# A linear-attention kernel with routed experts: the second copy of one head by a transfer of its own, for units 3 to 7

## The chip, the cores and the metric

The kernel runs on one core of a Trainium2 chip, in one launch. The metric is the device time of the whole program in microseconds (us). Beside the times there is a profile: one execution recorded by the hardware profiler. The engines are called as in its rows: PE (TensorE's matmuls) and PEld (its weight loads), DVE (VectorE), ACT (ScalarE), POOL (GpSimd) and SP (SyncE, which here only issues transfers). A "q" behind a name (SPq, PEldq) marks an entry of that engine's sequencer, such as the issue of a transfer or a wait on a semaphore.

## What is computed

An RWKV-5 attention over 4 batches, 8 heads, 768 steps and 48 channels a head, and behind it a mixture of 8 experts in which every expert gets the same number of tokens:

```python
for t in range(S):
    kt, vt, rt = (k[:, :, t], v[:, :, t], r[:, :, t])
    cur = np.einsum('bhd,bhe->bhde', u[None] * kt, vt)
    y[:, :, t] = np.einsum('bhd,bhde->bhe', rt, state + cur)
    state = w[None, :, :, None] * state + np.einsum('bhd,bhe->bhde', kt, vt)
...
logits = x @ w_gate                      # x: y as 3072 rows of 384
order = np.argsort(-logits.flatten())    # best pairs of token and expert first
...                                      # a token takes the expert while it has room (384 places)
h = np.maximum(x[mask] @ w1[e], 0.0)     # 384 -> 1024
out[mask] = h @ w2[e]                    # 1024 -> 384
```

All data are float32. `r` stands for the receptances, `k` for the keys, `v` for the values, `w` for the decays.

## The kernel before, in words

The attention is done in 24 units: a unit is one batch and one chunk of 128 steps, and the units go chunk by chunk, four batches (`B` = 4) in each. The class `Mild` does this part, and the order of its work is written out by hand in `run`: step `n` of its loop does the main work of unit `n` and prepares units `n+1` to `n+5`. Each engine, and each queue of transfers, works its instructions off in that order.

Keys and receptances lie in `krs`, a ring of five buffers. A buffer holds ten places of 64 channels for each of the two (`H + 2` places, 48 of the 64 channels used): places 0 to 7 are the eight heads, and place 8 (`H`) holds a second copy of head 4 (`HP`). The helper `pair` makes pairs of heads for the transposes on PE: places (0,1), (2,3), (5,6) and (7,8). So the fourth pair needs the second copy, and PE's transposes of a unit end with it. POOL's product of the keys with the decays (`keys`, line 436, into `kss`) reads places 0 to 3 and 5 to 8, so it needs the second copy of the keys too; POOL's product of receptances and keys (`own`, lines 442 and 443, into `rk`) reads places 0 to 7 alone.

The steps that the change and the prediction touch:

- `load(n, what)`, line 336: SP issues one transfer for the keys, receptances or values of a unit, 128 rows of 8 heads, 192 bytes each, 192 KB. `start` issues those of units 0 to 4 (values: 0 to 3) ahead of everything; step `n` begins with the keys and receptances of unit `n+5` and the values of unit `n+4`.
- `again_one(n, x)`, line 344: ACT copies head 4 of a unit's keys (x = 0) or receptances (x = 1) into place 8. It is used for units 0 to 7: for units 0 to 2 ahead of the loop, for units 3 to 7 in steps 0 to 4. From unit 8 on, `again` (line 340) does the same for both on DVE.
- `diagonal` (line 495): ACT writes the diagonal of a unit's matrix `AT`, eight small instructions a unit; `own_sum` (line 448, DVE) sums what it writes.
- `turn(n)`: PE transposes the (scaled) keys and the receptances (line 458); ACT copies the one (line 475), DVE scales the other (line 477).
- `pairs` (line 505): 32 matmuls of keys against receptances into `g_ps`, and the masked copy of them on DVE (line 512).
- `outputs`: matmuls into `y_ps` (line 545), `keep` (line 524) for the state, and ACT's copy of the result (line 564). `rows` transposes a result (line 595), ACT copies it (line 604), and SP stores it (line 605).
- `gate_weights` (line 404): in step 2, behind the loads of that step, SP issues two transfers of 6 KB that bring the gate's weights `wgp`. They are first read in step 4 by `gate` (line 575), PE's product of the four results of a chunk with these weights; it comes behind `pairs` of that step and ahead of `outputs`.

Behind the attention, the tokens are assigned to experts by a search on DVE, gathered by POOL, and sent through the experts' two layers by PE.

Of the kernel before, what the change touches and what calls it, by code (L numbers as in the profile page):

```python
# [21 lines left out]
T = 128  # L22
# [4 lines left out]
def attention_any(ctx, tc, r, k, v, w, u, wg, x_dram, LG, ident, walk):  # L27
# [52 lines left out]
    nc.scalar.dma_start(u_bc, u.rearrange("h d -> (h d)").partition_broadcast(128))  # L80
    nc.scalar.dma_start(wg_sb, wg.rearrange("(f p) e -> p f e", p=128))
    load(0)
    load(1)

    pw = const.tile([128, HP, T], F32, name="pw")
# [54 lines left out]
    def scale(n):  # L140

        load(n + 2)
        kt, rt, vt = loaded.pop(n)
        c = units[n][1]
# [130 lines left out]
class Mild:  # L275
# [52 lines left out]
    def load(self, n, what):  # L328
        if n >= self.N:
            return  # L330
        nc, H, D = self.nc, self.H, self.D
        b, c = self.units[n]
        for x in what:
            t = self.vts[:, n % self.NV] if x == "v" else self.krs[:, n % self.NK, "kr".index(x)]
            src = {"k": self.k, "r": self.r, "v": self.v}[x]
            nc.sync.dma_start(t[:, 0:H, 0:D], src[b, :, ts(c, T), :].rearrange("h s d -> s h d"))

    def again(self, n):
        kr, HP, H, D = self.krs[:, n % self.NK], self.HP, self.H, self.D
        self.nc.vector.tensor_copy(kr[:, :, H, 0:D], kr[:, :, HP, 0:D])  # L340
# [278 lines left out]
    def run(self, step):  # L619
        N, B, C, walk = self.N, self.B, self.C, self.walk  # L620
        self.live = {n: {} for n in range(N)}
        self.start()
        u_ps = self.spread_u()
        self.again_one(0, 0)
        k0 = self.keys_turned(0, True)
        self.again_one(0, 1)
        self.idle(2, "g_ps")
        r0 = self.r_turned(0)
        self.copy_u(u_ps)
        self.own(0)  # L630
        self.scaled(0, "k", k0, "pieces")
        self.scaled(0, "r", r0, "pieces")
        self.table(self.WK, "k")
        self.again_one(1, 0)
        self.table(self.WR, "r")
        self.again_one(1, 1)
        self.idle(2, "g_ps")
        k1 = self.keys_turned(1, True, walk.ps, "few")
        wk_ps = self.wk_turned()
        r1 = self.r_turned(1, walk.ps, "counts")  # L640
        self.wk_table(wk_ps)
        self.scaled(1, "k", k1, self.WK)
        self.own_sum(0)
        self.diagonal(0, (0,))
        self.again_one(2, 0)
        self.diagonal(0, (1,))
        self.again_one(2, 1)
        self.scaled(1, "r", r1, self.WR)
        self.own(1)
        self.keys(0)  # L650
        self.own_sum(1)
        nc, AB = self.nc, self.ones8
        nc.vector.tensor_mul(self.chunk, AB[:, 0, :, 1, 8], AB[:, 0, :, 1, 8])
        self.pairs(0)
        self.diagonal(1)
        self.own(2)
        chores = walk.constants()
        for n in range(N):
            self.load(n + 5, "kr")
            self.load(n + 4, "v")  # L660
            if n == 2:
                self.gate_weights()
            soon, split, full = n <= B, 0 < n < 3, n >= B and n % B == 0
            halves = ((0,), (1,)) if split or full else ((0, 1), ())
            if n == 0:
                self.turn(2, True)
                self.own_sum(2)
                self.idle(3, "y_ps")
                self.pairs(1)
                self.keys(1)  # L670
            else:
                step(n, "first")
                if not soon and n + 3 < N:
                    self.again(n + 3)
                if n == 2:
                    self.own_sum(n + 2)
                if split:
                    self.keep(n - 1)
                    self.pairs(n + 1)
                if n + 2 < N:  # L680
                    if n != 2 and n + 3 < N:
                        self.own_sum(n + 2)
                    self.turn(n + 2, between=lambda: step(n, "turning"))
                if n <= N - B:
                    self.rows((n - 1,), "few")
            if soon:
                self.again_one(n + 3, 0)
            if n + 2 < N:
                self.diagonal(n + 2, halves[0])
            if soon:  # L690
                self.again_one(n + 3, 1)
            if n > 2:
                step(n, "turned")
                if n <= B:
                    self.keep(n - 1)
                if n + 1 < N:
                    self.pairs(n + 1, lambda: step(n, "products"))
                step(n, "paired")
            if n + 3 < N:
                self.keys(n + 3)  # L700
                self.own(n + 3)
                if n == 1:
                    self.keys(2)
            if full:
                self.gate(n // B - 1, range(B))
                if n + 2 < N:
                    self.diagonal(n + 2, halves[1])
            if n == N - 1:
                rows = self.rows_turned((N - 4, N - 3), "g_ps", lambda: step(n, "rows"))
                self.rows_out((N - 4, N - 3), rows)  # L710
            self.outputs(n, lambda: step(n, "states"), (lambda: self.logits(n // B - 1)) if full else (lambda: None))
            if split:
                self.diagonal(n + 2, halves[1])
            if n == N - 4:
                self.own_sum(N - 1)
            step(n, "last")
            if n == 13:
                walk.guess_most(self.LG[:, 0:3 * B, :], AX.XY)
            if n == 14:
                walk.guess(walk.ps.tile([128, 128], F32, name="most_ps", tag="few"), self.ident)  # L720
            if n == N // 2 + 1:
                for _ in chores:
                    pass
                self.test()
            if n > 2:
                for _ in range(6):
                    next(chores, None)
        self.gate(C - 1, range(B - 1))
        one = self.rows_turned((N - 2,), "kT_ps")
        self.gate(C - 1, [B - 1])  # L730
        last = self.rows_turned((N - 1,), "g_ps")
        self.logits(C - 1)
        return one, last
# [1285 lines left out]
```

## Time and profile before

| | us |
|---|---|
| median of 3 runs | 394.56 (394.26 to 394.99) |
| the profiled execution | 393.36 |
| its span, first to last instruction | 391.6 |
| PE busy | 377.2 (96%) |
| PEld busy | 306.2 (78%) |
| DVE busy | 281.4 (72%) |
| ACT busy | 169.3 (43%) |
| POOL busy | 141.2 (36%) |

The shares are means over the whole span. The attention's part is the first third of it; there ACT and POOL are far fuller than their means say, and so are the transfers: the slices of about 10 us that cover the first 90 us show the 16 transfer engines at eight or nine tenths or more. A row of the timeline has the start, the length, the engine, the line of the kernel, the operation, what it writes and reads, the count of instructions merged into the row and, in brackets, the idle time of the engine ahead of it with what ended it. The length of an issue on SP is that of the issue, not of the transfer; "DMA to landing" is the time from the issue to the arrival of all its data.

### The profile page before, as it was taken

To read this page: it belongs to the slowest core of one execution; us is meant where nothing else is said; L and a number is where in the kernel's file an instruction comes from. 1 tells how busy PE (TensorE), PEld (TensorE's weight loads), DVE (VectorE), ACT (ScalarE), POOL (GpSimd) and SP (SyncE) were. 2 spreads that over 40 slices of the span, in tenths; PEclk is the share of its full clock that TensorE was granted. 3 is DMA by queue.
4 is the path that set the end of the run, shared out by engine and by line. 5 is a ranking of instruction groups with operands and counts; after the bars stand their busy time and mean duration, and the time that the engine had idled before them with its cause. 6 is when DMAs were issued, how large, how long until landed. Compare 5 with 4: busy or idle time off the path is not lost. (4 is left out here: it accounts for less than half of the span.)

```text
span 391.6 us, 9858 instructions
## 1 busy us (share of the span) xinstructions
PE 377.2 (96%) x3777; PEld 306.2 (78%) x3777; DVE 281.4 (72%) x959; ACT 169.3 (43%) x452; POOL 141.2 (36%) x173
## 2 busy tenths in 40 slices
PE   8899999999999999999999999999999999999992
PEld 7677888888877866687578899558657889989991
DVE  6755777586885788985949949888378976994530
ACT  4997989888883311312222242121222234234220
POOL 7878887767732022032122021203203212070020
PEclk9999999999999999999999999999999999999997
DMA  9999999988692164651560560109209264280010
GB/s 121 160 180 174 210 189 201 174 171 157 129 338 82 43 241 181 195 190 42 164 238 28 168 251 20 41 5 345 77 20 338 85 231 173 52 329 24 2 62 27
DMA packets 95335, 57.35 MB, mean 146 GB/s; under 512 B 77232, under 2 KB 89520, under 8 KB 95280
## 3 DMA queue, kind: packets, MB, share of 16 engines
q1 hardware_dynamic: 91936, 47.21, 48.0%
q0 software_dynamic: 3104, 9.44, 7.0%
q8 instruction: 31, 0.51, 0.6%
q14 instruction: 24, 0.20, 0.2%
q10 hardware_dynamic: 240, 0.00, 0.0%
HBM read 47.20 MB, written 9.44 MB: 145 GB/s over the span
## 5 line engine op out<-in xcount | busy, mean ns | idle before, releaser
L1624 PE MATMUL h_ps<-xT,w 128*128 128x384 f32 (+1 forms) x264 | 72.6, 427 | 0.0
L495 ACT ACTIVATE AT<-ident,dd 128x128 f32<-128x128 f32 x192 | 59.6, 392 | 2.2 <-DVE dd L448 2.1
L1624 PEld LDWEIGHTS h_ps<-xT,w 128*128 128x128 f32 x264 | 42.0, 191 | 19.6 <-issue 2.2
L1518 POOL DMA_INDIRECT xg<-x_rows,tok x22 | 22.5, 1021 | 92.4 <-PE h_ps L1624 23.7
L1750 POOL DMA_INDIRECT out_dram<-o_all,to x16 | 20.8, 1299 | 85.3 <-DVE o_all L1738 22.2
L1627 ACT ACTIVATE hid<-h_ps 128x384 f32<-128x384 f32 (+1 forms) x40 | 17.9, 449 | 54.2 <-PE h_ps L1624 50.9
L512 DVE COPY_PREDICATED AT<-mask,g_ps 64x512 f32<-64x512 uint8 (+1 forms) x48 | 32.4, 723 | 11.7 <-PE g_ps L505 9.9
L1756 PE MATMUL o_ps<-w,hid 128*128 128x384 f32 x96 | 32.5, 490 | 0.0
L505 PE MATMUL g_ps<-rT,kT 48*64 48x128 f32 (+1 forms) x768 | 26.3, 255 | 1.8 <-DVE AT L512 1.0
L436 POOL TENSOR_TENSOR kss<-krs,wk 128x384 f32<-128x384 f32 x24 | 24.3, 1016 | 8.0 <-DVE krs L340 5.0
L1756 PEld LDWEIGHTS o_ps<-w,hid 128*128 128x128 f32 x96 | 17.7, 190 | 10.6 <-issue 0.5
L545 PE MATMUL y_ps<-AT,vts 128*64 128x128 f32 x384 | 25.7, 276 | 0.0
L443 POOL TENSOR_TENSOR rk<-rk,u_bc 128x384 f32<-128x384 f32 x24 | 24.1, 1003 | 1.9
L505 PEld LDWEIGHTS g_ps<-rT,kT 48*64 48x64 f32 x768 | 20.6, 132 | 5.1 <-PE unread_ps L418 0.9
L442 POOL TENSOR_TENSOR rk<-krs 128x384 f32<-128x384 f32 x24 | 24.5, 1022 | 0.2 <-DMA krs<-in_r_dram 0.2
L545 PEld LDWEIGHTS y_ps<-AT,vts 128*64 128x64 f32 x384 | 20.6, 137 | 1.0 <-issue 0.7
L477 DVE TENSOR_TENSOR rT<-rT_ps,WR 112x512 f32<-112x512 f32 x23 | 15.7, 683 | 4.2 <-PE rT_ps L458 4.2
L448 DVE TENSOR_REDUCE dd<-rk 128x8 f32<-128x384 f32 x24 | 13.1, 545 | 6.9 <-POOL rk L443 6.9
L564 ACT COPY x<-y_ps 128x512 f32<-128x512 f32 x24 | 14.1, 586 | 5.9 <-PE y_ps L545 5.0
L458 PE MATMUL rT_ps<-ident,krs 128*112 128x128 f32 x96 | 15.4, 281 | 0.5 <-DMA krs<-in_r_dram 0.4
L1698 PE MATMUL pa_ps<-T,S 128*128 128x192 f32 x80 | 15.8, 331 | 0.0
L1729 PE MATMUL p_ps<-W,H 128*128 128x128 f32 x128 | 15.8, 275 | 0.0
(340 smaller groups left out, 834.2 us busy)
## 6 DMA issues: line engine op xcount, KB each, us to landing
w<-in_moe_w_dram SPq DMA_DIRECT2D x18, 1536.0 KB, 8.7
krs<-in_k_dram SPq DMA_DIRECT2D x24, 192.0 KB, 4.5
krs<-in_r_dram SPq DMA_DIRECT2D x24, 192.0 KB, 4.8
vts<-in_v_dram SPq DMA_DIRECT2D x24, 192.0 KB, 4.9
x_rows<-xr SPq DMA_DIRECT2D x24, 192.0 KB, 3.5
xg<-x_rows,tok POOLq DMA_INDIRECT x22, 4.0
out_dram<-o_all,to POOLq DMA_INDIRECT x16, 2.7
out_dram<-o_sb,to POOLq DMA_INDIRECT x5, 4.7
```

The lines of the kernel that those rows point to most:

```text
L436: self.nc.gpsimd.tensor_mul(self.kss[:, n % self.NS].rearrange("p (g h) d -> p g h d", g=2)[:, :, :, 0:D], src, self.wk.rearrange("p (g h) ...
L442: nc.gpsimd.tensor_mul(rk, self.krs[:, n % self.NK, 1, 0:H, 0:D], self.krs[:, n % self.NK, 0, 0:H, 0:D])
L443: nc.gpsimd.tensor_mul(rk, rk, self.u_bc)
L495: nc.scalar.mul(AT[:, z, a, :], self.ident, dd[:, h:h + 1])
L505: nc.tensor.matmul(g_ps[ts(i, PD), z, a, i * PD:], kT[rows, a, ts(i, PD)], rT[rows, a, i * PD:], start=True, stop=True)
L512: nc.vector.copy_predicated(out=AT[keys, :, :, steps], mask=mask, data=g_ps[keys, :, :, steps])
L545: nc.tensor.matmul(yv[q * PD:(q + 1) * PD, o // 2, o % 2, :], lhsT, rhs, start=(o // 2, q) not in seen, stop=stop, skip_group_check=True)
L1518: nc.gpsimd.indirect_dma_start(out=xg[:, c, :], out_offset=None, in_=x_dram[0:within, :], in_offset=bass.IndirectOffsetOnAxis(ap=tok[:, c: ...
L1624: nc.tensor.matmul(h_ps[j][:, at], w1[:, f, ts(j, 128)], xT[:, f, at], start=(f == 0), stop=(f == KD - 1))
L1627: nc.scalar.activation(hid[:, j, 0:m], h_ps[j][:, 0:m], AF.Relu)
L1750: nc.gpsimd.indirect_dma_start(out=to, out_offset=bass.IndirectOffsetOnAxis(ap=tok, axis=0), in_=o_sb, in_offset=None)
L1756: nc.tensor.matmul(o_ps, hid[:, j, ts(c, 128)], w2[:, j, :], start=(j == 0), stop=(j == KF - 1))
```

## The change

For units 3 to 7, `load` issues a second, small transfer behind each one of keys or receptances: head 4 of the same unit, 128 rows of 192 bytes (24 KB), from the same tensor into place 8. The two ACT copies in steps 0 to 4, which wrote place 8 for these units, are taken out. The places of units 0 to 2 and of unit 8 and later are written as before.

```diff
@@ load
             nc.sync.dma_start(t[:, 0:H, 0:D], src[b, :, ts(c, T), :].rearrange("h s d -> s h d"))
+            if x != "v" and 3 <= n <= self.B + 3:
+                nc.sync.dma_start(t[:, H, 0:D], src[b, self.HP, ts(c, T), :])
@@ run
-            if soon:
-                self.again_one(n + 3, 0)
             if n + 2 < N:
                 self.diagonal(n + 2, halves[0])
-            if soon:
-                self.again_one(n + 3, 1)
             if n > 2:
```

So the loads of units 3 and 4 in `start` become eight transfers in place of four, and those that steps 0, 1 and 2 issue for units 5, 6 and 7 become twelve in place of six. `soon` is true in steps 0 to 4.

## The prediction

> **What bounds the kernel now.** I read four views: the busy time of the engines by stretches of 10 us, then what TensorE waited for, then the order of time on PE, POOL, ACT and SP between 9 and 36 us, last the transfers with their landings. The stretches come first, because the removed copies all lie before 34 us (columns: stretch, length, then PE, PEld, DVE, ACT and POOL busy with their counts, granted clock, DMA share, GB/s):
>
> ```profile
> 10.00:20.00 10.00, 8.24 (x155) 6.59 (x157) 7.79 (x15) 9.01 (x32) 8.26 (x9) 1.00 1.41 155
> 20.00:30.00 10.00, 9.08 (x169) 7.68 (x165) 5.83 (x12) 10.00 (x34) 8.40 (x9) 1.00 1.11 185
> 30.00:40.00 10.00, 9.74 (x205) 7.91 (x205) 5.22 (x11) 7.77 (x26) 8.51 (x20) 1.00 0.92 182
> 40.00:50.00 10.00, 10.00 (x217) 9.00 (x216) 8.22 (x23) 9.24 (x27) 8.86 (x15) 1.00 1.11 206
> ```
>
> From 40 us on PE has no gap: whatever it has lost or won by then stays to the end. Before that it idles 1.76, 0.92 and 0.26 us per stretch, ACT is full from 20 to 30 us, and the DMA share is near 1 or over it. So two things are short at the place of the change: ACT, which the change relieves, and the transfers, to which it adds. The question is which of them PE is held by, place by place. The waits on PE's path and POOL's rows:
>
> ```profile
> POOL kss L436 <- ACT krs L344: 3.0, 3, 1.9
> PE kT_ps L458 <- POOL kss L436: 0.9, 1, 0.9
> PE x_ps L595 <- ACT x L564: 0.2, 1, 0.2
> PEld lg_ps L575 <- issue: 0.3, 1, 0.3
> 17.70 1.00 POOL L443 TENSOR_TENSOR rk<-rk,u_bc 128x384 f32<-128x384 f32 x1
> 20.56 1.02 POOL L436 TENSOR_TENSOR kss<-krs,wk 128x384 f32<-128x384 f32 x1 [1.87 <-ACT krs L344]
> 25.62 0.65 PE L458 MATMUL kT_ps<-ident,kss 128*112 128x128 f32 x4 [0.85 <-POOL kss L436]
> 30.44 0.82 PE L458 MATMUL rT_ps<-ident,krs 128*112 128x128 f32 x4
> 31.41 0.60 PE L595 MATMUL x_ps<-ident,x 112*128 112x112 f32 x4 [0.16 <-ACT x L564]
> 32.55 1.10 PE L505 MATMUL g_ps<-rT,kT 48*64 48x128 f32 x32
> 33.72 0.84 PEld L575 LDWEIGHTS lg_ps<-x,wgp 128*32 128x32 f32 x32 [0.31 <-issue]
> ```
>
> The reader is to see a chain: POOL's scaled keys of unit 4 start at 20.56 after 1.87 us of idling for an ACT copy; POOL then runs unit 4's and unit 5's work without a break, and PE stands 0.85 us at 25.62 for unit 5's scaled keys. That chain is what the change is aimed at. And a second place, easily missed: PE's first gate product (line 575) starts at 33.72 after an idle time that the view calls issue. Its operand `wgp` comes by two small transfers that SP issues in step 2. Their rows, first both together, then the second alone, with the wait that PE makes for them, and the transfer of v of unit 6 ahead of them:
>
> ```profile
> L404 SPq DMA_DIRECT2D wgp<-in_moe_w_gate_dram x2: 434/623/812, 28.4 to 29.3; - x2
> DMA to landing us min/median/max: 4.3/4.7/5.0
> L404 SPq DMA_DIRECT2D wgp<-in_moe_w_gate_dram x1: 434/434/434, 29.3 to 29.3; - x1
> DMA to landing us min/median/max: 4.3/4.3/4.3
> L575 PEldq EVENT_SEMAPHORE  x1: 51/51/51, 33.6 to 33.6; - x1
> 27.65 0.73 SPq L336 DMA_DIRECT2D vts<-in_v_dram  x1
> DMA to landing us min/median/max: 5.6/5.6/5.6
> 28.43 1.30 SPq L404 DMA_DIRECT2D wgp<-in_moe_w_gate_dram  x2
> ```
>
> The first lands at 28.43 + 5.0 = 33.43, the second at 29.3 + 4.3 = 33.6; PE's semaphore wait ends at 33.6 and the weight load follows at 33.72. The matmuls before it began at 32.55, and 32 of them take 1.03 us from first start to the next group's (17.34 to 18.36 in unit 2's place, where the next group follows at once):
>
> ```profile
> 17.34 1.10 PE L505 MATMUL g_ps<-rT,kT 48*64 48x128 f32 x32 [0.32 <-DVE AT L512]
> 18.36 0.65 PE L458 MATMUL kT_ps<-ident,kss 128*112 128x128 f32 x4
> ```
>
> So PE was ready at about 33.57 and the gate weights came at 33.6: today they are just in time, with no slack. This place decides what reaches the end.
>
> **The change, part by part.** Removed: ten ACT copies (units 3 to 7, keys and receptances; the other six of the row below stay).
>
> ```profile
> L344 ACT COPY krs<-krs x16: 213/228/243, 5.3 to 33.7; 128x48 f32<-128x48 f32 x16
> 30.65 0.23 ACT L344 COPY krs<-krs 128x48 f32<-128x48 f32 x1
> 30.77 0.59 ACT L564 COPY x<-y_ps 128x512 f32<-128x512 f32 x1
> ```
>
> A copy holds ACT's queue for 0.12 us (30.65 to 30.77), ten of them 1.2 us. What PE gets of it directly is the 0.16 at 31.41 and 0.17 in the group at 30.44 (0.82 against the 0.65 of the group at 25.62).
>
> Moved: POOL's scaled keys no longer wait for ACT but for the small transfer. Unit 4's keys, issued at 13.10, land 6.7 us later, at 19.80:
>
> ```profile
> L336 SPq DMA_DIRECT2D krs<-in_k_dram x1: 1312/1312/1312, 13.1 to 13.1; - x1
> DMA to landing us min/median/max: 6.7/6.7/6.7
> ```
>
> So of POOL's 1.87 us only 0.76 (19.80 to 20.56) belongs to ACT; the rest is the transfer itself. With three small transfers ahead of or at that point (keys and receptances of unit 3, keys of unit 4), priced below at 0.15, the second copy is there at 20.25, POOL starts at about 20.35, and its chain gains 0.2 us. When what ACT gives at 31.41 is added, PE reaches the gate product about 0.4 us sooner, at 33.2. If each small transfer cost 0.43 there, POOL would start at 21.1 and PE would lose 0.5 instead. Neither matters to the sum, as the next step shows.
>
> Added: ten transfers of 24 KB (128 rows of 192 bytes) on SP's queue, each right behind its large one. All ten stand in SP's order ahead of the gate weights: the last two, for unit 7, are issued in the same step as `wgp` and before it. Their readers' waits (the old unit's transposes and POOL's products) are those of the large transfers, long past, so no new stall of SP comes from there. Is SP's queue free to take them? Its rows:
>
> ```profile
> 9.56 1.14 SPq L336 DMA_DIRECT2D krs<-in_k_dram  x1
> 10.75 1.14 SPq L336 DMA_DIRECT2D krs<-in_r_dram  x1
> ...
> 19.38 0.89 SPq L336 DMA_DIRECT2D krs<-in_r_dram  x1
> ...
> 23.12 2.22 SPq L336 DMA_DIRECT2D vts<-in_v_dram  x1
> 25.43 0.90 SPq L605 DMA_DIRECT2D x_rows<-xr  x1
> 26.44 0.38 SPq L336 DMA_DIRECT2D krs<-in_k_dram  x1
> 26.90 0.65 SPq L336 DMA_DIRECT2D krs<-in_r_dram  x1
> ```
>
> It issues without a pause, and at the pace of the engines: 192 KB each 1.19 us (9.56 to 10.75), so the queue is backed up and what is put in moves everything behind it. A small transfer has an eighth of the rows of a large one: 1.19 / 8 = 0.149 for the four before 16 us, 0.60 together. From 19.38 to 23.12 four large ones take 3.74, 0.935 each, an eighth of which is 0.117. The two gate transfers, the only other small ones in that queue, landed 0.17 apart (33.43, 33.60). For the six later ones I take 0.125, nearer to the row of the same 192-byte kind, 0.75 together. Sum: 1.35 us later for all that follows, `wgp` too.
>
> Bounds of this unknown: the nearest rows give no price for a 24 KB transfer alone. Below: if eight of the ten hide in the moments in which SP was blocked for 2.22 us with one issue, the two of unit 7 remain, 2 x 0.43 of issue time, less the 0.62 by which the issues at 26.90 and 27.65 exceed the shortest (0.65 + 0.73 - 2 x 0.38): 0.25 us. Not below nothing, for nothing is taken out of SP's queue. Above: each costs a whole issue slot of its own, 0.43 (the second gate transfer's 434 ns): ten make 4.3.
>
> The Trainium skill, page "DMA: Bandwidth & Descriptors", section "Rules for kernel authors", says to coalesce many small transfers into a large one, since under 64 KB one pays mostly overhead; its bandwidth table has 0.68 us for 4 KB and 0.95 for 64 KB. By these figures ten transfers one after another would come to an estimated 7 to 9.5 us; no row here shows a single 24 KB load, and the two landings 0.17 us apart disagree with so high a price in a full queue.
>
> The sum: the second gate transfer lands at 33.60 + 1.35 = 34.95 and PE's gate product starts at about 35.07, 1.35 us after 33.72, though PE is ready at 33.2. PE's gain of 0.4 us before it is waited away. Behind it PE runs without gaps, so the 1.35 stay. The loads that follow are late by the same amount as PE, and keep their distance; the DVE copies for unit 8 and later, which need whole loads, are untouched. In the profiled execution: 393.36 (its span 391.6 and 1.76 around it) + 1.35 = 394.71. That execution lies 1.20 below the median of 394.56, so the forecast for the median is 395.9.
>
> **The rivals.** Faster: the added transfers cost nothing in the queue and the gate weights come sooner than now. For it speak POOL's 1.87 and PE's 0.85; the most PE could win before the gate product is 0.85 at 25.62, 0.17 at 30.44 and 0.16 at 31.41, 1.2 in all, so 393.4. Against it: even if `wgp` landed exactly when it does today, PE would wait until 33.6 as now and win nothing; it decides only from a landing 0.8 us earlier on, and ten issues are put ahead of it, none removed. Chance 0.06.
>
> No change to be told: the ten ride in the gaps that the engines have while SP is blocked, `wgp` is late by 0.25 (the lower bound) and PE with it: 394.8. For it speaks that the stretch 30 to 40 has a DMA share of 0.92. Against it, the share of 1.11 to 1.41 in the 20 us before, and SP's rows, in which no issue up to 28 us waits for anything but the queue itself. It covers delays up to 0.79. Chance 0.23.
>
> Slower by more: from 16.9 us on, where SP isn't only waiting for room, each small one costs its slot: 0.60 + 6 x 0.43 = 3.2 us, 397.7; with all ten, 398.9. Against it: an issue that waits for room anyway hides its own length. The page named above points this way. Chance 0.13.
>
> **How the numbers follow.** The forecast (a delay of the gate weights between 0.8 and about 2.2 us) has 0.58. A measurement of this kernel tells about 0.2%, 0.79 us, from no change: slower 0.58 + 0.13 = 0.71, same 0.23, faster 0.06. The range goes from 394.7, near the lower bound, to 397.8, which takes in the six slots.
>
> **What would show it.** Right: the ten ACT copies gone, POOL's scaled keys of unit 4 start between 20.2 and 20.6, SP's issue of `wgp` stands near 30 us instead of 28.43, it lands near 35, PE's line 575 begins at about 35 with an idle time of 1.5 us or more before it, and from 40 us on PE is as full as now. Wrong: if line 575 begins before 34.3 (the small transfers are nearly free), if PE's 0.85 at 25.62 grows past 1.5 (they are dear already for unit 4), or if PE makes up the delay after 40 us, where I see no gap for it.

## The result, and the profile after

| | before | after | ratio, 95% interval |
|---|---|---|---|
| median, first chip | 394.64 us (394.26 to 394.99) | 396.74 us (395.70 to 398.55) | 1.0061 (1.0047 to 1.0074) |
| median, another chip | 393.72 us (393.09 to 394.40) | 395.45 us (394.83 to 396.98) | 1.0047 (1.0035 to 1.0059) |
| profiled execution, its span (first chip) | 393.36, 391.6 | 396.50, 394.8 | |

The changed kernel is slower, by 0.0061 x 394.64 = 2.4 us (1.9 to 2.9) on one chip and 0.0047 x 393.72 = 1.9 us (1.4 to 2.3) on another; the medians lie 2.1 and 1.7 us apart. The ratios, here and below, are estimated from the executions in the chip's usual state (so one of a3's ten, at 2144.55 us, is out of its ratio) and aren't quotients of the medians. On the first chip its times also spread wider: 2.85 us from lowest to highest against 0.73.

The stretches of after, in the columns of the prediction (length, PE, PEld, DVE, ACT, POOL, granted clock, DMA share, GB/s):

```profile
20.00:30.00 10.00, 9.41 (x171) 7.91 (x169) 5.85 (x12) 9.32 (x28) 8.84 (x9) 1.00 0.79 155
30.00:40.00 10.00, 7.90 (x155) 6.54 (x153) 4.78 (x11) 6.29 (x19) 6.53 (x17) 1.00 0.97 184
40.00:50.00 10.00, 10.00 (x232) 8.92 (x232) 7.33 (x20) 9.00 (x26) 8.87 (x16) 1.00 1.01 195
```

From 20 to 30 us PE is 0.33 us busier than before (9.41 against 9.08) and ACT is no longer full (9.32 against 10.00). From 30 to 40 us PE loses 1.84 (7.90 against 9.74). So PE was indeed given something first, and more was taken from it behind that. The waits of after's first 42 us (engine, tile and line, what it waited for: us, times, longest) and PE's and POOL's rows at those places:

```profile
POOL kss L438 <- DMA krs<-in_k_dram: 3.0, 2, 1.9
PE lg_ps L577 <- DMA wgp<-in_moe_w_gate_dram: 1.5, 1, 1.5
PE x_ps L597 <- ACT x L566: 0.6, 1, 0.6
PE kT_ps L460 <- POOL kss L438: 0.5, 1, 0.5
...
20.56 1.02 POOL L438 TENSOR_TENSOR kss<-krs,wk 128x384 f32<-128x384 f32 x1 [1.88 <-DMA krs<-in_k_dram]
25.63 0.65 PE L460 MATMUL kT_ps<-ident,kss 128*112 128x128 f32 x4 [0.51 <-POOL kss L438]
31.62 0.60 PE L597 MATMUL x_ps<-ident,x 112*128 112x112 f32 x4 [0.57 <-ACT x L566]
32.76 1.10 PE L507 MATMUL g_ps<-rT,kT 48*64 48x128 f32 x32
35.39 1.08 PE L577 MATMUL lg_ps<-x,wgp 128*32 128x128 f32 x32 [1.53 <-DMA wgp<-in_moe_w_gate_dram]
```

In before the gate product and ACT's rows at this place were:

```profile
33.75 1.08 PE L575 MATMUL lg_ps<-x,wgp 128*32 128x128 f32 x32
28.17 0.24 ACT L344 COPY krs<-krs 128x48 f32<-128x48 f32 x1
28.30 2.46 ACT L495 ACTIVATE AT<-ident,dd 128x128 f32<-128x128 f32 x8
```

The gate product begins at 35.39 instead of 33.75, 1.64 us later, and the wait ahead of it names the gate's weights. Two smaller lines are as telling. POOL's keys of unit 4 still start at 20.56 after the same idle time: only the name of what they wait for has changed, from ACT's copy to a transfer. And PE's 0.16 us ahead of the transposes of a result (now line 597) has become 0.57. ACT's rows of after say why:

```profile
28.65 2.45 ACT L497 ACTIVATE AT<-ident,dd 128x128 f32<-128x128 f32 x8 [0.38 <-DVE dd L450]
31.01 0.56 ACT L566 COPY x<-y_ps 128x512 f32<-128x512 f32 x1
```

Where a copy of line 344 stood in before, ACT now waits 0.38 us for DVE's sum `dd`, which is made of POOL's product. The eight diagonal instructions start at 28.65 instead of 28.30, and the copy of `x` behind them at 31.01 instead of 30.77. POOL's product of unit 5, of which `dd` is made, starts later too. Its rows in before and after:

```profile
25.52 1.01 POOL L442 TENSOR_TENSOR rk<-krs 128x384 f32<-128x384 f32 x1
25.95 1.00 POOL L444 TENSOR_TENSOR rk<-krs 128x384 f32<-128x384 f32 x1 [0.38 <-DMA krs<-in_r_dram]
```

It waits for the unit's receptances, a load that now has small transfers ahead of it. The same wait, 0.50 to 0.68 us, stands in b1, c1 and a3 below, all with ten transfers, and in no kernel with six or fewer (a1, with ten too, waits 0.79 there, which the view puts down to DVE). So at this place the transfers take back what the missing copies give ACT.

SP's issues around the gate's weights in after (start, length):

```profile
29.66 0.39 SPq L336 DMA_DIRECT2D krs<-in_r_dram  x1
30.09 0.70 SPq L338 DMA_DIRECT2D krs<-in_r_dram  x1
30.89 1.53 SPq L336 DMA_DIRECT2D vts<-in_v_dram  x1
32.47 1.06 SPq L406 DMA_DIRECT2D wgp<-in_moe_w_gate_dram  x2
```

SP reaches `wgp` at 32.47, 4.04 us later than before (28.43), while PE gets it 1.64 later. Behind the gate product nothing is made up or lost for a long time. The same two matmuls in before (first pair of rows) and after (second pair):

```profile
36.85 0.33 PE L585 MATMUL lt_ps<-ident,lg 128*128 128x128 f32 x1
121.08 0.18 PE L1430 MATMUL list_ps<-e_both,alike 128*128 128x8 f16 x1
```

```profile
38.49 0.33 PE L587 MATMUL lt_ps<-ident,lg 128*128 128x128 f32 x1
122.73 0.18 PE L1428 MATMUL list_ps<-e_both,alike 128*128 128x8 f16 x1
```

1.64 late at the first, 1.65 at the second, 84 us on. (The two profiled executions differ by 3.14 us, more than the medians: before's lies 1.3 below its own median. By PE's last `list_ps`, at 348.03 in before, the distance is 2.66. But in b1 below, the changed kernel once more, the distance is 3.08 at the first `list_ps` and 3.27 at the last, and c2, whose median is that of before, falls 0.74 further behind from `lt_ps` to the last, so I take the rest to belong to single executions and not to the change.) The start of `lt_ps`, the transposes of the gate's result, is the mark used below for every kernel: 36.85 in before. Differences of 0.3 us between two single executions say little: a2 and c4 below differ from before, up to the pairs ahead of the gate product, only in when the gate's weights are issued, and these pairs start at 32.84 and 32.86 in them, at 32.55 in before's profile.

### The profile page after: what moved, and what is told of

It reads as the page before. It is cut to its first block, busy times and chain, and to the rows that moved or that the text cites. A ratio compares the mean times of both kernels' runs of the same rounds, so it can differ in the third digit from the quotient of the medians.

```text
span 394.8 us, 9859 instructions
## 1 busy us (share of the span) xinstructions
PE 378.7 (96%) x3777; PEld 307.3 (78%) x3777; DVE 281.6 (71%) x959; ACT 167.8 (43%) x442; POOL 141.1 (36%) x173
## 4 chain that ended last, share of the span: by engine, by line
PE 69%; DVE 9%; issue 9%; POOL 5%; DMA 4%; ACT 2%; POOLq 0%; another core or an unknown queue 0%; SPq 0%; DVEq 0%
PE h_ps L1622 14%; PE pa_ps L1696 7%; PE o_ps L1754 7%; PE y_ps L547 5%; PE h_ps L1599 4%; PE g_ps L507 4%; PE pb_ps L1696 3%; PE hb_ps L1599 3%; PE e_h_ps L1847 3%; PE kT_ps L460 2%; PE x_ps L597 2%; PE kv_ps L526 2%; PE pc_ps L1696 2%; PE rT_ps L460 2%; PE xT_ps L1531 2%
```

## The experiments

The theory under test: the loss is the lateness of the gate's weights behind the ten transfers, and nothing else. The main rival was that the small transfers, or the loss of ACT's copies, cost time in the loop itself (POOL's chain, later loads). A second question was whether the relief of ACT is worth anything once the gate's weights are out of the way. Where a kernel built on before has more lines, its numbers differ by one to three.

**The gate's weights first, with and without the change.** The two transfers of `gate_weights` go out in `start`, on ACT's queue, instead of in step 2 on SP's: `a1_gate_first` is after with this edit, `a2_before_gate_first` is before with it.

```diff
+        self.gate_weights()                     # in start
...
-            self.nc.sync.dma_start(self.wgp[z * PD:z * PD + self.D, :, 0:self.E],
+            self.nc.scalar.dma_start(self.wgp[z * PD:z * PD + self.D, :, 0:self.E],
...
-            if n == 2:
-                self.gate_weights()
```

> The changed kernel, with the two gate-weight transfers issued at the very start on ACT's queue instead of in step 2 on SP's. Theory (the ten small transfers cost time only because the gate weights stand behind them on SP): the wait of 1.53 us at line 575 is gone, the gate product follows the 32 matmuls within 1.1 us, and the time falls from 396.7 to between 394.2 and 395.0, the kernel before give or take 0.4. Rival (the transfers slow POOL, DVE and PE all along, the gate wait only shows it): PE loses the 1.6 us elsewhere before 45 us and the time stays at 396 or above.

> The kernel before, with only the same move of the gate weights. Theory (they land just in time there, at 33.6 us against a PE ready at 33.57): next to nothing, 394.2 to 394.7. Rival (the gate weights cost the kernel before something too): faster than 394.0.

Measured against before on the same chip: a1 394.69 us to 394.68, ratio 0.9998 (0.9990 to 1.0007); a2 394.66, ratio 1.0002 (0.9993 to 1.0010). The change with all its ten transfers costs nothing once the gate's weights don't stand behind them. PE's rows in a1:

```profile
32.08 0.60 PE L598 MATMUL x_ps<-ident,x 112*128 112x112 f32 x4 [0.97 <-ACT x L567]
...
33.21 1.10 PE L508 MATMUL g_ps<-rT,kT 48*64 48x128 f32 x32
34.24 1.08 PE L578 MATMUL lg_ps<-x,wgp 128*32 128x128 f32 x32
```

The gate product follows the pairs at once (33.21 + 1.03 = 34.24). It isn't earlier than in before, though: the wait for ACT's copy of `x` has grown to 0.97.

**The transfers alone, and the absence of the copies alone.** `a3_transfers_alone` is before with ten such transfers, into memory that nothing reads; all copies stay. `a4_no_copies` is after without the ten transfers, so that nothing fills these places in units 3 to 7 (in two of the five buffers they are set to zero once, at the start).

```diff
+            if x != "v" and 3 <= n <= self.B + 3:          # a3, on before
+                nc.sync.dma_start(self.spare[:, (2 * n + "kr".index(x)) % 5, :], src[b, self.HP, ts(c, T), :])
...
-            if x != "v" and 3 <= n <= self.B + 3:          # a4, on after
-                nc.sync.dma_start(t[:, H, 0:D], src[b, self.HP, ts(c, T), :])
```

> The kernel before with all its ACT copies, plus the ten small transfers in the same places of SP's order, into spare space that nothing reads. Theory: the gate weights are as late as in the changed kernel, the time is 396 to 397.2. Rival (the loss comes from POOL and PE waiting for the small transfers where they waited for ACT): nothing waits for these, so the time stays within 0.4 of 394.6.

> The ten ACT copies taken out and nothing put in their place: head 4's second copy of units 3 to 7 is left out, so that part isn't computed from the right data. Theory: what ACT and POOL gain is waited away at the gate weights, which land when they did, at 33.6 us; 394.2 to 394.7. Rival (ACT's queue is what bounds PE up to 34 us): the 1.2 us of the copies come off, 393.4.

a3: 395.84 us against 394.68, ratio 1.0030 (1.0020 to 1.0040), so +1.2 us. a4: 394.43, ratio 0.9996 (0.9987 to 1.0005). The gate product of a3, then PE's rows of a4:

```profile
34.98 1.08 PE L578 MATMUL lg_ps<-x,wgp 128*32 128x128 f32 x32 [1.03 <-DMA wgp<-in_moe_w_gate_dram]
```

```profile
31.89 1.10 PE L506 MATMUL g_ps<-rT,kT 48*64 48x128 f32 x32
33.34 1.08 PE L576 MATMUL lg_ps<-x,wgp 128*32 128x128 f32 x32 [0.36 <-DMA wgp<-in_moe_w_gate_dram]
```

Without any copy being touched, the ten transfers make a loss of 1.2 us, with 1.23 of after's 1.64 us at the gate product; the time lies just under the 396 that was expected. Without copies and without transfers PE is at the pairs 0.66 us sooner than in before (31.89 against 32.55) and gives 0.25 of it back at once, by waiting for the gate's weights: what the prediction called waited away.

**The same without either.** `b3_no_copies_gate_first` is a4 with the gate's weights first: nothing of the change's costs, and neither of the two places where its gain was lost. The same part is left out.

> The ceiling: no copies, no transfers (the second copy of head 4 of units 3 to 7 is left out) and the gate weights at the start on ACT's queue. Theory (with the gate weights out of the way, PE keeps what POOL and ACT give it): the gate product starts at about 33.0, 0.3 to 0.4 earlier than without the move, the time is 393.7 to 394.1. Rival (what is gained here is lost behind): 394.4 or more.

393.41 us against 393.72, ratio 1.0001 (0.9992 to 1.0009). A miss: I had expected a gain that can be told. PE's rows:

```profile
31.38 0.60 PE L597 MATMUL x_ps<-ident,x 112*128 112x112 f32 x4 [0.59 <-ACT x L566]
...
32.51 1.10 PE L507 MATMUL g_ps<-rT,kT 48*64 48x128 f32 x32
33.54 1.08 PE L577 MATMUL lg_ps<-x,wgp 128*32 128x128 f32 x32
```

With no copy, no transfer and no wait for weights, the gate product starts 0.21 us earlier than in before (33.54 against 33.75). At line 597 PE waits 0.59 for ACT's copy of `x`, as in after and a1. In a4 that wait was 0.16 and PE at the pairs 0.62 sooner than here. But b3's execution is behind a4's from the beginning: here are the pairs of step 0 in before, a4 and b3.

```profile
14.45 1.10 PE L505 MATMUL g_ps<-rT,kT 48*64 48x128 f32 x32 [0.71 <-DVE AT L512]
14.21 1.10 PE L506 MATMUL g_ps<-rT,kT 48*64 48x128 f32 x32 [0.70 <-DVE AT L513]
15.00 1.10 PE L507 MATMUL g_ps<-rT,kT 48*64 48x128 f32 x32 [0.70 <-DVE AT L514]
```

This start varies from execution to execution (14.80 in after, 14.15 in b1, which is the same kernel). Counted from it, PE reaches the pairs ahead of the gate product after 18.10 us in before (18.11 in a2 and c4), after 17.68 in a4 and 17.51 in b3. So without transfers the missing copies bring PE there 0.4 to 0.6 us sooner. With the ten transfers it is 17.96 in after, 18.02 in c1 and 18.37 in b1: little or nothing is left of it. Neither a4's nor b3's time shows a gain that can be told.

**Part of the transfers.** `b2_units_3_4` has the four for units 3 and 4 on before, `c2_unit_7` the two for unit 7, `c3_units_5_7` the six for units 5 to 7; the copies that they replace are taken out, the others stay. `b4_keys_4_6_gate_first` tries for a faster kernel: the keys of units 4 and 6 alone, the gate's weights first.

```diff
+            if x != "v" and n in (3, 4):        # c2: n == 7; c3: n in (5, 6, 7); b4: x == "k" and n in (4, 6)
+                nc.sync.dma_start(t[:, H, 0:D], src[b, self.HP, ts(c, T), :])
```

> A smaller dose: transfers for units 3 and 4 alone (four, all ahead of the loop), the copies of units 5 to 7 stay on ACT, the gate weights stay in step 2. By the prediction's price of 0.15 each the gate weights land 0.6 us later, PE's line 575 starts at 34.3, the time is 395.1 to 395.4. If a transfer costs a whole issue slot of 0.43: 1.7 us later, 396.3. If the queue makes up the four before step 2: no change, within 0.3 of 394.6.

> Transfers only where POOL waited for ACT, the keys of units 4 and 6; all other copies stay on ACT; the gate weights at the start on ACT's queue. Theory: with no small transfer ahead of unit 4's keys POOL starts its product at 20.0 to 20.2 instead of 20.56, PE's wait of 0.85 us for unit 5 falls to 0.4 or less, the gate product starts about 0.5 earlier, the time is 394.0 to 394.3. Rival (the small transfer lands so late behind the large one that POOL gains nothing): POOL at 20.5 or later and 394.5 to 395.

> The two transfers of unit 7 alone, which are the last ahead of the gate weights; the copies of units 3 to 6 stay on ACT. By issue slots (two of 0.43 to 1.0 us right ahead, with the queue nearly empty): the gate weights land 0.5 to 1.0 us later, the time is 0.4 to 1.0 above the kernel before. By the prediction's 0.125 each: 0.25 later, no change to be told.

> The six transfers of units 5 to 7; the copies of units 3 and 4 stay on ACT. As the four of units 3 and 4 alone cost nothing, theory: the whole loss comes from these six, the gate weights are as late as in the changed kernel and the time is 1.4 to 2.4 us above the kernel before. Rival (the price is per transfer): six tenths of it, 0.9 to 1.3.

| kernel | transfers ahead of `wgp` | SP issues `wgp` at | gate product at | median, before's | ratio |
|---|---|---|---|---|---|
| before (profile) | 0 | 28.43 | 33.75 | | |
| c2_unit_7 | 2 | 29.30 | 33.92 | 394.67, 394.67 | 1.0000 (0.9991 to 1.0009) |
| b2_units_3_4 | 4 | 29.28 | 33.87 | 393.72, 393.72 | 1.0006 (0.9997 to 1.0015) |
| c3_units_5_7 | 6 | 30.81 | 34.78 | 395.44, 394.67 | 1.0026 (1.0014 to 1.0038) |
| after | 10 | 32.47 | 35.39 | 396.74, 394.64 | 1.0061 (1.0047 to 1.0074) |

b4 came to 393.53 us, ratio 1.0003 (0.9991 to 1.0014): no gain; POOL's keys of unit 4 start at 20.38 in it, between what the theory and the rival had put. In c2 and b2 the gate product follows the pairs without a wait; their 0.17 and 0.12 come from the pairs, which start at 32.89 and 32.84, as they do in a2 and c4 without any transfer. In b2 the weights are issued 0.85 us later than in before and land no later, from a row of its `wgp` issues:

```profile
L406 SPq DMA_DIRECT2D wgp<-in_moe_w_gate_dram x2: 434/636/838, 29.3 to 30.2; - x2
DMA to landing us min/median/max: 3.4/3.7/4.1
```

29.28 + 4.1 = 33.4 and 30.2 + 3.4 = 33.6, the landings of before. So the price is not a sum over transfers: at the gate product two cost nothing that can be seen (in c2 a landing up to 33.92 would be hidden), four nothing, six 1.0 us, ten 1.2 in a3 and 1.5 to 1.6 in b1, c1 and after. The theory that c3 put first, that the whole loss comes from the six late ones, did not hold at the size it gave: they make 1.03 of 1.64. Its rival, a price per transfer, fits c3 taken by itself, but not the four of b2, for which it would give 0.6. Why the four early ones are free alone and worth 0.2 to 0.6 on top of the six stays open. One reading, not tested: now and then, mostly five to eight us apart, an issue on SP takes 1.4 to 3.0 us, in all of these kernels. One of them starts in after at 30.89 (1.53 us, above), and one in before at 30.79:

```profile
30.79 1.92 SPq L336 DMA_DIRECT2D krs<-in_r_dram  x1
```

In before the gate's weights are out by then; in after they stand behind it, and in c3 their own first issue lasts 1.98.

**The weights late, without any transfer added.** `c4_gate_late` is before with the gate's weights issued one step later.

```diff
-            if n == 2:
+            if n == 3:
                 self.gate_weights()
```

> The kernel before, with the gate weights issued one step later and nothing else changed: about 5 us later in SP's order, landing near 37.5 instead of 33.6. It makes the wait without any of the transfers. Theory: PE stands for 3.5 to 4 us, its clock falls to 0.50 behind it in every execution, and the time is 5 to 5.5 us above the kernel before. Without the fall of the clock it would be 3.5 to 4. Rival (PE makes up a late gate product behind it): 2 us or less.

399.32 us against 394.67, ratio 1.0115 (1.0100 to 1.0131), some 4.5 us. The order of cause is confirmed: this one position is enough to make the kernel slower. The size falls short of what was expected, for the weights came sooner (wait 2.57), and it has two parts. The row of the wait, and the stretches behind it:

```profile
36.53 1.90 PE L575 MATMUL lg_ps<-x,wgp 128*32 128x128 f32 x32 [2.57 <-DMA wgp<-in_moe_w_gate_dram]
...
37.00:38.00 1.00, 1.00 (x27) 0.97 (x20) 0.00 (x0) 0.00 (x0) 0.00 (x0) 0.50 1.04 199
38.00:39.00 1.00, 1.00 (x21) 0.64 (x16) 0.00 (x0) 0.53 (x3) 0.00 (x0) 0.50 1.36 206
39.00:40.00 1.00, 1.00 (x24) 0.67 (x16) 0.00 (x0) 0.91 (x4) 0.00 (x0) 0.50 1.27 210
```

The gate product starts 36.53 - 33.75 = 2.78 late, and then takes 1.90 us instead of 1.08: the granted clock is at 0.50 for some 3.4 us (the stretches of 1 us ahead of these and behind have 0.82 and 0.98). `lt_ps` starts at 41.18, 4.33 late, so the clock adds 1.55 to the wait. That it falls in every execution, as expected, one profile can't show; the four times lie within 0.83 us.

**After again, and with PE kept busy.** Does the same happen in the changed kernel? `b1_after_again` is after, unedited, on another chip. `c1_filler` is after with twelve matmuls whose result nobody reads, on PE between the pairs of step 4 and the gate product.

```diff
+                if n == B:
+                    self.idle(12, "y_ps")       # 12 transposes of a constant, not read
```

> The changed kernel once more, with a new profile. Open: its first profile starts the gate product 1.64 us later than the kernel before, but ends 3.2 us later, with further losses of 0.7 us at 126 us and 0.5 us at 381 us in places that the change does not touch. If those belong to single executions: 396.0 to 396.4 (1.3 to 1.8 above before), and the new profile has them elsewhere or not at all. If they belong to this program: 396.7 or more, and the profile shows them at the same places.

> The changed kernel with twelve matmuls whose result nobody reads on PE right ahead of the first gate product, about 1.5 us of work at the 0.12 us of the transposes around it. They fill the wait for the gate weights. Theory (the change costs 1.6 us by the late gate weights, and in some executions another 1.4 us, because PE's granted clock falls to 0.50 for 3 us after standing still, as the second profile of the changed kernel shows from 36 to 39 us): the clock stays at 1.00, the executions lie closer together, and the median is 1.3 to 1.9 us above the kernel before. Rival (the clock falls for another reason): the median is 2 us or more above, and the clock falls in some profiles as before.

b1's rows and stretches, then after's stretch at the same place:

```profile
31.39 0.60 PE L597 MATMUL x_ps<-ident,x 112*128 112x112 f32 x4 [0.89 <-ACT x L566]
35.28 1.67 PE L577 MATMUL lg_ps<-x,wgp 128*32 128x128 f32 x32 [1.66 <-DMA wgp<-in_moe_w_gate_dram]
...
36.00:37.00 1.00, 1.00 (x23) 0.62 (x19) 0.00 (x0) 0.01 (x1) 0.14 (x1) 0.50 1.15 226
37.00:38.00 1.00, 1.00 (x18) 0.67 (x19) 0.00 (x0) 1.00 (x4) 0.00 (x0) 0.50 1.08 162
38.00:39.00 1.00, 1.00 (x20) 1.00 (x20) 0.00 (x0) 0.43 (x2) 0.00 (x0) 0.50 1.29 243
39.00:40.00 1.00, 1.00 (x19) 0.83 (x16) 0.92 (x3) 0.00 (x0) 0.49 (x2) 0.99 1.05 229
```

```profile
36.00:37.00 1.00, 1.00 (x35) 0.63 (x25) 0.00 (x0) 0.47 (x3) 0.28 (x1) 1.00 1.15 218
```

In one execution of the same kernel the clock stays at 1.00, in the other it falls to 0.50 for 3.4 us (35 to 36 us has 0.81); `lt_ps` starts at 38.49 in the one and 39.91 in the other, 1.64 and 3.06 after before's. b1's gate product is 1.53 late, so the clock adds 1.53. Its median is 1.7 above before's, in the range that was expected if after's further losses belong to one execution. With the filler the clock was 1.00 in every stretch from 35 to 39 us, as it was in after's profile without it:

```profile
33.83 1.53 PE L420 MATMUL unread_ps<-ident 128*128 128x128 f32 x12
35.34 1.08 PE L577 MATMUL lg_ps<-x,wgp 128*32 128x128 f32 x32
```

c1's times: 396.30 us (395.94 to 396.88) against 394.67, ratio 1.0044 (1.0031 to 1.0058), so 1.7 us, near the 1.59 by which its gate product is late. After's ratios gave 2.4 and 1.9. The filler's interval overlaps both, so a saving isn't shown; its five times spread over 0.94 us, against 2.85 (eight) and 2.15 (six) for after, as was expected if the clock falls in some executions without it.

The same comparison for every kernel, the lateness of `lt_ps` in its one profiled execution beside the ratio's difference in us, shows how far this one place carries the result: a3 1.23 and 1.2; c3 1.03 and 1.0; c1 1.59 and 1.7; c4 4.33 and 4.5; b2 0.12 and 0.2; c2 0.17 and 0.0; a2 0.12 and 0.1; b3 -0.21 and 0.0; a1 0.49 and -0.1; a4 -0.40 and -0.2; after 1.64 and 2.4; after again 3.06 and 1.9. The odd one is b4, 1.30 and 0.1, whose profiled execution, at 394.73, is 1.2 above its own median. Two of its stretches and the row of POOL's keys of unit 5 show why:

```profile
15.00:16.00 1.00, 1.00 (x28) 1.00 (x26) 1.00 (x3) 0.85 (x4) 1.00 (x2) 0.50 1.52 164
17.00:18.00 1.00, 1.00 (x13) 1.00 (x11) 1.00 (x2) 1.00 (x4) 1.00 (x2) 0.50 1.45 174
26.10 1.01 POOL L439 TENSOR_TENSOR kss<-krs,wk 128x384 f32<-128x384 f32 x1 [1.69 <-ACT krs L346]
```

The clock fell here too, for 3.4 us from 14.8 on, ACT came late to its copy for unit 5, and POOL's keys of this unit waited for it. PE's waits ahead of that fall were 0.51, 0.56 and 0.69 us, with nothing but transposes between them; before has 0.29, 0.39 and 0.71 at this place and keeps its clock. For the rest one place explains the times to 0.25 us, but for a1 (0.6), after, and after again, whose profiled executions lie below and above their medians.

## Why the prediction was right, and where its sizes were off

The forecast, slower by 1.35 us at 395.9, named the place, the wait and the sign, and the time, 396.74, came inside its range. That the sum came as near as it did is in part luck, since its parts were off. Point by point:

- **The place holds.** The gate product's weight load began at 35.36 for a predicted 35.07, after a wait for `wgp` of 1.53 us. That PE has no slack there holds for before's profiled execution alone: in a2 and c4 PE would be ready at about 33.88, 0.3 behind the 33.6 at which the weights landed in before. Moving these weights removes the whole loss (a1), making them late without the change makes one (c4).
- **No gain from ACT's relief holds, for partly other reasons.** Waited away it is, but not only at the gate. The 20.35 at which POOL was to start came out at 20.56 in after, as in before, and at 20.00 in b1: no clear gain. And the 0.4 us by which PE was to be ready sooner, at 33.2, wasn't there: it was ready at 32.76 + 1.03 = 33.79, since POOL waits for unit 5's receptances and ACT for `dd`, and copies `x` later. The relief by itself was sized about right, 0.4 to 0.6 us in a4 and b3; what failed is that the working let the small transfers delay unit 4's keys and `wgp`, and no other load. The faster rival's "1.2 in all" was too high a ceiling: even without any of the costs PE gains 0.6 (b3). In after the first of its three stalls shrinks from 0.85 to 0.51, and the last grows from 0.16 to 0.57, behind `dd`.
- **The term of the sum that was mis-sized: 0.60 + 0.75 for the queue.** The sum came out at 1.64 (1.53, 1.59 and, with the copies kept, 1.23 in b1, c1 and a3) instead of 1.35, so 0.12 to 0.16 a transfer, near the 0.149 and 0.125 taken from the large ones. But its parts are not what the two terms say: the first four alone cost 0 (b2), not 0.60, and the six alone 1.03 (c3), not 0.75. An eighth of a large one's time was a fair mean price for ten, and adding it up per transfer was not a fair model. The bounds, 0.25 and 4.3, held what ten transfers cost at the gate product.
- **SP's issue of `wgp` "near 30 us" failed** (32.47). The working took issue and landing to move together. The issue moved by 4.04 (3.90 in b1), the landing by 1.6 (33.6 to 35.2 in b1), for the time from issue to landing shrank: 4.3 to 5.0 us before, in after again:

```profile
L406 SPq DMA_DIRECT2D wgp<-in_moe_w_gate_dram x2: 434/504/574, 32.3 to 33.0; - x2
DMA to landing us min/median/max: 2.2/2.5/2.7
```

- **A term was missing: the clock.** The wait was priced at its own length. In an execution where it ends in a drop of the granted clock (b1), 1.53 us come on top, 3.06 - 1.53. That fits a median above the 1.64 of the quiet execution and the wide spread. How often it happens, and so how much of the 1.9 to 2.4 it makes, is open, as only two executions of this kernel were profiled. There is a hint in the mean granted clock of each execution: after's three longest (397.71 to 398.55) have 0.990 to 0.993 and b1's longest (396.98) 0.990, all others of the two 0.994 to 0.998. In both runs the first group's mean lies 1.5 us above the second's, which is itself 1.8 and 1.7 above before's median. A mean doesn't say where the clock fell, and the groups were made afterwards. The Trainium skill, page "TensorE: Matmul & The Clock Gate", section "Part 1: The HAM clock gate (the "warmup" mystery)", has PE fall to half clock after an idle window of about 3.4 us, and this window runs freely. The half clock is what the rows show; but here PE idled only 1.66 us at a stretch in b1, with 0.89 three microseconds ahead of it, 2.57 in c4, and no more than 0.69 in b4. That one execution with 1.53 kept its clock and one with 1.66 lost it would suit a limit that depends on the position in such a window; no run here separates the two.
- **"PE makes up nothing behind 40 us" holds** to 0.01 us over 84 us.
- **The slower rivals** (3.2 and 4.3 for full issue slots) are out as a mechanism: the issues did take such slots, 4.04 in all, and PE paid only 1.64. The rival of no change would have needed a landing not later than 0.79; it holds for two and for four transfers, not for ten.

No variant was faster than before. The cheapest repair of the change, a1, is equal to it.

## What to carry to other kernels

Before small loads are put into a queue, look down the order of that queue for the small, late-bound load that some engine waits for, and move it to the front or to another queue: here two transfers of 6 KB decided over the whole change. Work taken off a full engine is worth only what its next wait allows: follow the engine's next instruction to its operand (here `dd`), and that to the load behind it, which the change itself may delay, before booking a gain. And price a new wait on PE with what the clock may do behind it, not with its length alone.

## What the runs showed of the hardware that I had not expected

- A wait of PE of 1.66 us (b1) and of 2.57 us (c4) was followed by a granted clock of 0.50 for 3.4 us, which cost 1.53 and 1.55 us more; one of 1.53 us (after) was not. In b4 the clock fell for as long behind waits of at most 0.69 us.
- A load issued 0.85 us later landed at the same time (b2), and one issued 4.04 us later was used 1.64 later (after): the moment of issue alone doesn't tell the landing.
- The cost of added transfers of 24 KB in a full queue was not proportional at the place that waited for the load behind them: nothing to be seen for two and for four, 1.0 us for six, 1.2 to 1.6 us for ten.
